# The first forward stage on four 64x64 tiles of the TensorE array, with retuned slots, table rows from PSUM and a last store in halves

## The chip, the cores and the metric

One core of a Trainium2 chip runs the kernel. The metric is device time in microseconds, the median of several executions. Ratios are the mean time of one kernel's runs over that of the other's in the same rounds, so they are not quite the ratio of the medians quoted beside them.

## The reference

```python
X = np.fft.rfft(x, axis=1)                       # x: (8, 3008, 256)
y = np.fft.irfft(X * (filt_r + 1j*filt_i), n=3008, axis=1)
h = y.reshape(24064, 256) @ w_in                 # to 2048
out = (0.5*h*(1 + erf(h/sqrt(2)))) @ w_out       # back to 256
```

The FFT of 3008 = 47 x 64 points is four stages of small matmuls with two trips through DRAM (R1 after the first stage, R2 after the third). The two large matmuls are called ps_h (L450) and ps_o (L464).

## The kernel before: what the argument touches

PSUM is the memory that TensorE writes its results to; it is handed out in banks. Time is planned in slots. A slot holds one ps_h pair (two matmuls of 512 columns) and four ps_o matmuls (256 columns each). The FFT stages of batch b are laid into the slots ahead of hi, the slot in which the large matmuls first need that batch.

```python
def s1(self, b, u):                       # first forward stage, u = 0..15, one a slot
    ...
    ps = self.bank("ps_s1")               # pool "f": 3 PSUM banks for all stages
    nc.tensor.matmul(ps[0:96, :], lhsT=self.T1, rhs=self.st[b, "x"][:, 2*u:2*u+2, :],
                     start=True, stop=True)
    i = (u % 4) * 2
    self._evac(a[:, i:i + 2, :].rearrange("p a b -> p (a b)"), ps[0:96, :], False)   # DVE
    if u % 4 == 3:
        ...                               # two DMAs of a_sb to R1, 192 KB each
...                                       # (cut)
s1, n1, r1, s2, n2, r2, s4, n4 = hi - 94, 1, hi - 78, hi - 69, 3.7, hi - 23, hi - 17, 1
#  s1 first stage; r1 read b_sb from R1; s2 second stage (s3 four slots behind it);
#  r2 read d_sb from R2; s4 last inverse stage
...                                       # (cut)
m.psum(ctx, h=(3, 1), o=(2, 1), f=(3, 1)) # eight banks in all
```

T1 is 94x96 and block diagonal: two halves of the input, 47 rows each, give 48 outputs each, and the other half of the weights is zero.

## Time and profile before

| | before |
|---|---|
| time | 785.1 us (4 runs, 784.36 to 785.24) |
| span of the profiled execution | 781.9 us |
| TensorE busy / share of the last chain | 98% / 93% |
| first forward stage, batches 1 to 7 | 112 matmuls, 220 ns each between starts |
| holes ahead of the last inverse stage | 3.2 us in six batches |

In the views PE is TensorE, PEld its weight loads, DVE VectorE, ACT ScalarE, POOL GpSimd, and SPq the queue from which SyncE issues DMAs. A line has the start, the length, the engine, the line of the kernel, the operation, output<-inputs, the shape and the count; brackets give the idle time just before it and what ended that. A hole is a stretch in which TensorE waits.

The prediction below shows the lines for this. The first is the order of time of the weight loads. The second is the waits: who waited for whom, us in total, times, longest.

```profile
117.50 0.12 PEld L261 LDWEIGHTS <-T 94*96 94x96 bf16 x1
117.72 0.54 PEld L464 LDWEIGHTS <-g_sb 128*128 128x128 bf16 x4
118.27 0.21 PEld L450 LDWEIGHTS <-w_in_sb 128*128 128x128 bf16 x2
```

```profile
PE ps_s L334 <- DMA d_sb<-R: 2.2, 3, 1.8
```

The weights of the first-stage matmul are loaded at 117.50 for a matmul that starts at 117.72. They come one matmul ahead and cost nothing. The wait for d_sb is the only one that TensorE has in the long part.

### The profile page before, as it was taken

The page shows a single profiled execution, that of the slowest core. Times are in us where ns is not written, and L with a number is a line of the kernel's source. Part 1 is how long each engine was busy: PE and PEld are TensorE (multiplying, and loading weights), DVE is VectorE, ACT ScalarE, POOL GpSimd, SP SyncE. Part 2 cuts the span into 40 slices and gives each one's busy share as a digit, 9 for nine tenths or more (in the row PEclk, how much of TensorE's full clock was granted, in tenths as well). Part 3 has the DMA queues.
Part 4 walks back from the last instruction along what each step waited for, and adds up shares of the span by engine and source line. Part 5 has one row for each costly group of instructions (what it writes and reads, how often), then busy time and mean ns, then how long its engine had stood idle before and what let it go on. Part 6 is the DMA issues. An engine that isn't in the chain of part 4 may idle for free.

```text
span 781.9 us, 14728 instructions
## 1 busy us (share of the span) xinstructions
PE 769.3 (98%) x5938; PEld 538.1 (69%) x5938; DVE 403.1 (52%) x720; ACT 567.5 (73%) x978; POOL 64.7 (8%) x155
## 2 busy tenths in 40 slices
PE   8899999999999999999999999999999999999997
PEld 5857676676777766677677776667767677766666
DVE  8866756464554645556454664546645366411011
ACT  6889855887558875588656986568965788666663
POOL 7801100020000100001000110001100000000000
PEclk9999999999999999999999999999999999999999
DMA  9784744465244761546615465254642521410111
GB/s 149 140 179 118 152 123 107 133 134 125 69 109 131 138 149 40 133 130 118 159 44 160 105 123 136 61 168 94 122 135 68 150 81 55 135 41 28 41 42 54
DMA packets 86213, 85.63 MB, mean 110 GB/s; under 512 B 5761, under 2 KB 76417, under 8 KB 86145
## 3 DMA queue, kind: packets, MB, share of 16 engines
q1 hardware_dynamic: 77760, 68.70, 31.0%
q0 software_dynamic: 8384, 16.00, 14.3%
q8 instruction: 46, 0.75, 0.4%
q14 instruction: 23, 0.18, 0.1%
HBM read 54.00 MB, written 46.66 MB: 129 GB/s over the span
## 4 chain that ended last, share of the span: by engine, by line
PE 93%; DMA 3%; POOL 1%; DVE 1%; ACT 0%; issue 0%; SPq 0%; POOLq 0%; DVEq 0%
PE ps_o L464 41%; PE ps_h L450 41%; PE ps_s L261 3%; PE ps_s L334 3%; PE ps_s L309 2%; PE ps_s L284 2%; DMA d_sb<-R 1%; DMA F<-in_filt_i_dram 1%; DMA x_sb<-in_x_dram 1%; PE ps_c3t L413 0%; DMA R<-v_sb 0%; POOL x_sb L82 0%; PE ps_c L427 0%; POOL T L201 0%; ACT vt_sb L246 0%
## 5 line engine op out<-in xcount | busy, mean ns | idle before, releaser
L453 ACT ACTIVATE g_sb<-ps_h 128x512 bf16<-128x512 f32 x752 | 439.1, 596 | 190.3 <-PE ps_h L450 179.5
L464 PE MATMUL ps_o<-w_out_sb,g_sb 128*128 128x256 bf16 x3008 | 449.1, 272 | 0.0
L450 PE MATMUL ps_h<-y_sb,w_in_sb 128*128 128x512 bf16 (+3 forms) x1600 | 447.6, 366 | 0.5 <-DVE y_sb L250 0.5
L464 PEld LDWEIGHTS <-g_sb 128*128 128x128 bf16 x3008 | 287.6, 98 | 133.8
L450 PEld LDWEIGHTS <-w_in_sb 128*128 128x128 bf16 x1600 | 154.9, 98 | 23.3 <-issue 0.8
L468 DVE COPY ost<-ps_o 128x512 f32<-128x512 f32 x94 | 64.3, 684 | 125.2 <-PE ps_o L464 124.7
L292 DVE TENSOR_TENSOR p<-ps_s,F 128x512 bf16<-128x512 f32 x84 | 58.1, 691 | 103.5 <-ACT p L291 97.0
L250 DVE TENSOR_SCALAR y_sb<-ps_s 128x376 bf16<-128x376 f32 x112 | 60.9, 548 | 82.7 <-PE ps_s L334 82.7
L248 DVE CAST a_sb<-ps_s 96x512 bf16<-96x512 f32 x112 | 76.3, 686 | 40.8 <-PE ps_s L261 40.8
L248 DVE CAST v_sb<-ps_s 128x512 bf16<-128x512 f32 x84 | 57.5, 686 | 13.0 <-PE ps_s L309 13.0
L290 ACT ACTIVATE p<-ps_s 64x512 bf16<-64x512 f32 x84 | 49.8, 593 | 2.0
L334 PEld LDWEIGHTS <-d_sb 96*128 96x128 bf16 x448 | 30.3, 97 | 29.0 <-DMA d_sb<-R 3.3
L291 ACT CAST p<-ps_s 64x512 bf16<-64x512 f32 x84 | 48.5, 577 | 1.0
L101 POOL COPY gate<-p 1x1 bf16<-1x1 bf16 x48 | 8.5, 176 | 479.5 <-DVE p L294 479.5
L261 PE MATMUL ps_s<-x_sb,T 94*96 94x512 bf16 x112 | 42.7, 381 | 0.0
L334 PE MATMUL ps_s<-T,d_sb 96*128 96x94 bf16 x448 | 36.3, 204 | 2.3 <-DMA d_sb<-R 2.2
L294 DVE TENSOR_TENSOR p<-p 128x512 bf16<-128x512 bf16 x84 | 35.7, 425 | 2.9
L293 DVE TENSOR_TENSOR p<-p,F 128x512 bf16<-128x512 bf16 x84 | 34.9, 415 | 0.0
L82 POOL DMA_DIRECT2D x_sb<-in_x_dram x64 | 32.6, 515 | 13.0 <-issue 11.3
L309 PE MATMUL ps_s<-p,T 128*128 128x256 bf16 x168 | 32.1, 273 | 0.0
L284 PE MATMUL ps_s<-b_sb,T 128*128 128x256 bf16 x168 | 32.1, 273 | 0.0
L309 PEld LDWEIGHTS <-T 128*128 128x128 bf16 x168 | 16.3, 98 | 20.1 <-DVE p L294 0.5
(98 smaller groups left out, 191.1 us busy)
## 6 DMA issues: line engine op xcount, KB each, us to landing
out_dram<-ost SPq DMA_DIRECT2D x94, 256.0 KB, 2.5
x_sb<-in_x_dram POOLq DMA_DIRECT2D x64, 188.0 KB, 3.9
R<-a_sb SPq DMA_DIRECT2D x56, 192.0 KB, 3.0
b_sb<-R SPq DMA_DIRECT2D x28, 384.0 KB, 4.6
R<-v_sb SPq DMA_DIRECT2D x42, 256.0 KB, 4.0
d_sb<-R SPq DMA_DIRECT2D x56, 192.0 KB, 4.5
w_in_sb<-in_moe_w_in_dram POOLq DMA_DIRECT2D x2, 512.0 KB, 9.9
w_out_sb<-in_moe_w_out_dram POOLq DMA_DIRECT2D x2, 512.0 KB, 10.8
```

The lines of the kernel that those rows point to most:

```text
L248: self.nc.vector.tensor_copy(out=out, in_=in_)
L250: self.nc.vector.tensor_scalar(out=out, in0=in_, scalar1=scale, scalar2=None, op0=ALU.mult)
L261: nc.tensor.matmul(ps[0:96, :], lhsT=self.T1, rhs=self.st[b, "x"][:, 2 * u:2 * u + 2, :], start=True, stop=True)
L290: nc.scalar.activation(out=p2[0:64], in_=ps[64:128], func=AF.Copy, scale=-1.0)
L291: nc.scalar.copy(out=p2[64:128], in_=ps[0:64])
L292: nc.vector.tensor_tensor(out=p1, in0=ps, in1=f(0), op=ALU.mult)
L309: nc.tensor.matmul(ps[:, 256 * i:256 * i + 256], lhsT=self.T3[:, k].rearrange("p a b -> p (a b)"), rhs=w[:, 256 * i:256 * i + 256], start= ...
L334: nc.tensor.matmul(ps[:, 94 * i:94 * i + 94], lhsT=d[:, (grp % 2) * 4 + i, 128 * half:128 * half + 128], rhs=t4, start=True, stop=True)
L450: nc.tensor.matmul(ps[:, o:o + n], lhsT=self.w_in_sb[:, dc, jc * 128:jc * 128 + 128], rhs=self.ring[:, dc, off:off + n], start=(dc == 0), ...
L453: nc.scalar.activation(out=self.st["g", t][:, jc, :], in_=ps, func=AF.Gelu)
L464: nc.tensor.matmul(ps[:, tile_i % 2, :], lhsT=g[:, jc, tile_i * 128:tile_i * 128 + 128], rhs=self.w_out_sb[:, jc, :], start=(jc == 0), sto ...
L468: nc.vector.tensor_copy(out=ost, in_=ps)
```

## The change

The intent is to stop streaming over zeros: 47x48 blocks fit 64x64 tiles, four of which can work at once, so that four matmuls of 512 columns should take little more than one. The slots are retuned around it. Two small parts go with it: the negative table rows of the second half come out of PSUM on ScalarE instead of from GpSimd, and the last output tile is stored in two column halves.

```diff
     def s1(self, b, u):                        # now u = 0..7, one every two slots
+        ps = [self.bank("ps_s1") for h in range(2)]
+        c, i = u // 2, 2 * (u % 2)
+        for r in range(2):
             for h in range(2):
+                w = 8 * c + 4 * r + i
+                nc.tensor.matmul(ps[h][64 * r:64 * r + 64, :], lhsT=self.T1s[64 * h:64 * h + NA],
+                                 rhs=x[64 * h:64 * h + NA, w:w + 2, :], start=True, stop=True)
+        for h in range(2):
+            self._evac(a[:, h, i:i + 2, :].rearrange("p a b -> p (a b)"), ps[h], False)
...  (four DMAs of 96 KB in place of two of 192; x_sb at partitions 0 and 64; T1s built on GpSimd)
+            if h == 1:                         # table_2_swap: negative rows from PSUM
+                self._evac(t2[:, :, 0, 32 * i:32 * i + 32], ..., "act", 2.0 * i - 1.0)
...  (GpSimd copies filters 12 to 15 first, then the small tables, then filters 16 to 23)
+        if last and tile_i == 3:               # mm2: 16 matmuls of 128 columns, store, twice
...
-            s1, n1, r1, s2, n2, r2, s4, n4 = hi - 94, 1, hi - 78, hi - 69, 3.7, hi - 23, hi - 17, 1
+            s1, n1, r1, s2, n2, r2, s4, n4 = hi - 94, 1, hi - 78, hi - 71, 3.5, hi - 26, hi - 17, 1
```

More of the change, by code (lines that the diff above doesn't have):

```diff
@@ L76, in load_x @@
         if lo == 0 and 0 in hs:
-            self.st[b, "x"] = self.px.tile([2 * NA, HB, 256], BF16, tag="x", name="x_sb")
-        xt = self.st[b, "x"]
+            self.st[b, "x"] = self.px.tile([128 if b else 2 * NA, HB, 256], BF16, tag="x", name="x_sb")
+        xt, o = self.st[b, "x"], 64 if b else NA
         xv = self.x[b].rearrange("(n1 h c w) d -> h c n1 w d", h=2, c=4, w=8)
@@ L81, in load_x @@
             for h in hs:
-                nc.gpsimd.dma_start(out=xt[h * NA:(h + 1) * NA, c * 8:c * 8 + 8, :], in_=xv[h, c])
+                nc.gpsimd.dma_start(out=xt[h * o:h * o + NA, c * 8:c * 8 + 8, :], in_=xv[h, c])
     def load_filters(self, k0, k):
@@ L197, in table_2_swap, with table_2_minus @@
                        "act", 1.0 - 2.0 * i)
-    def table_2_minus(self, eng, h):
-        t2 = self.T2[:, 12 * h:12 * h + 12]
-        eng.tensor_scalar(out=t2[:, :, 0, :], in0=t2[:, :, 2, :], scalar1=-1.0, scalar2=None, op0=ALU.mult)
+            if h == 1:
+                self._evac(t2[:, :, 0, 32 * i:32 * i + 32], ps[:, 0:384].rearrange("p (k j) -> p k j", k=12),
+                           "act", 2.0 * i - 1.0)
+    def table_2_minus(self):
+        t2 = self.T2[:, 0:12]
+        self.nc.vector.tensor_scalar(out=t2[:, :, 0, :], in0=t2[:, :, 2, :], scalar1=-1.0, scalar2=None, op0=ALU.mult)
     def weights_4(self, g):
@@ L250, in _evac, with table_1_tiles @@
             self.nc.vector.tensor_scalar(out=out, in0=in_, scalar1=scale, scalar2=None, op0=ALU.mult)
+    def table_1_tiles(self, g):
+        v = self.nc.gpsimd
+        self.T1s = g.tile([128, 64], BF16, name="T1s")
+        v.memset(self.T1s, 0.0)
+        for r in (0, 64):
+            v.tensor_copy(out=self.T1s[r:r + NA, 0:48], in_=self.T1[0:NA, 0:48])
     def s1(self, b, u):
         nc = self.nc
-        if u % 4 == 0:
-            self.st[b, "a"] = self.pa.tile([96, 8, 256], BF16, tag="a", name="a_sb")
+        if u % 2 == 0:
+            self.st[b, "a"] = self.pa.tile([128, 2, 4, 256], BF16, tag="a", name="a_sb")
         if u == 0:
             self.st[b, "R1"] = self.dram.tile([NB, 48, 256], BF16, tag="R1", name="R1")
-        a, R1 = self.st[b, "a"], self.st[b, "R1"]
-        ps = self.bank("ps_s1")
-        nc.tensor.matmul(ps[0:96, :], lhsT=self.T1, rhs=self.st[b, "x"][:, 2 * u:2 * u + 2, :],
-                         start=True, stop=True)
-        i = (u % 4) * 2
-        self._evac(a[:, i:i + 2, :].rearrange("p a b -> p (a b)"), ps[0:96, :], False)
-        if u % 4 == 3:
-            c = u // 4
-            w = R1.rearrange("n q c -> q n c")
-            for h in range(2):
-                nc.sync.dma_start(out=w[:, h * HB + c * 8:h * HB + c * 8 + 8, :],
-                                  in_=a[h * 48:h * 48 + 48, :, :])
+        a, R1, x = self.st[b, "a"], self.st[b, "R1"], self.st[b, "x"]
+        ps = [self.bank("ps_s1") for h in range(2)]
+        c, i = u // 2, 2 * (u % 2)
+        for r in range(2):
+            for h in range(2):
+                w = 8 * c + 4 * r + i
[3 more added lines that the diff above has]
+            self._evac(a[:, h, i:i + 2, :].rearrange("p a b -> p (a b)"), ps[h], False)
+        if u % 2 == 1:
+            o = R1.rearrange("n q c -> q n c")
+            for r in range(2):
+                for h in range(2):
+                    w = HB * h + 8 * c + 4 * r
+                    nc.sync.dma_start(out=o[:, w:w + 4, :], in_=a[64 * r:64 * r + 48, h])
     def r1(self, b, c):
@@ L457, in mm2 @@
         tile_i, q = s // 4, s % 4
+        g = self.st["g", t]
+        last = t == self.B * self.S // TCH - 1
+        if last and tile_i == 3:
+            half = q // 2
+            if q % 2 == 0:
+                self.st["o"] = self.bank("ps_e", "o")
+            ps = self.st["o"][:, 0:128]
+            for jc in range(8 * (q % 2), 8 * (q % 2) + 8):
+                nc.tensor.matmul(ps, lhsT=g[:, jc, 384:512], rhs=self.w_out_sb[:, jc, 128 * half:128 * half + 128],
+                                 start=(jc == 0), stop=(jc == 15))
+            if q % 2 == 1:
+                self.store(t, 3, ps, slice(128 * half, 128 * half + 128))
+            return
         if s % 8 == 0:
@@ L460, in mm2 @@
         ps = self.st["o"]
-        g = self.st["g", t]
         for i in range(4):
@@ L465, in mm2 @@
                              rhs=self.w_out_sb[:, jc, :], start=(jc == 0), stop=(jc == 15))
-        if s % 8 == 7:
+        if last and s == 11:
+            self.store(t, 2, ps[:, 0, :], slice(0, 256))
+        elif s % 8 == 7:
             ost = self.po.tile([128, 2, 256], FP32, tag="ost", name="ost")
@@ L470, in mm2, with store @@
             nc.sync.dma_start(out=self.out[r0:r0 + 256, :].rearrange("(s p) o -> p s o", p=128), in_=ost)
+    def store(self, t, tile_i, ps, cols):
+        ost = self.po.tile([128, 2, 256], FP32, tag="ost", name="ost")
+        o = ost[:, 0, 0:cols.stop - cols.start]
+        self.nc.vector.tensor_copy(out=o, in_=ps)
+        r0 = t * TCH + tile_i * 128
+        self.nc.sync.dma_start(out=self.out[r0:r0 + 128, cols], in_=o)
 @with_exitstack
@@ L520 @@
     m.dup_filters(nc.gpsimd, 4, 8)
-    m.T1p = g.tile([2 * NA, 2, K1, 2], BF16, name="T1p")
-    nc.gpsimd.tensor_copy(out=m.T1p, in_=m.T1.rearrange("p (h r k) -> p h k r", h=2, r=2))
-    m.T1q = g.tile([2 * NA, K1, 2, 2], BF16, name="T1q")
-    nc.gpsimd.tensor_copy(out=m.T1q, in_=m.T1.rearrange("p (h r k) -> p k r h", h=2, r=2))
     warm = g.tile([128, 1], FP32, name="warm")
@@ L534 @@
             m.table_2_swap(0)
-            m.table_2_minus(nc.vector, 0)
+            m.table_2_minus()
             m.warm_up(3)
@@ L552 @@
             m.table_2_swap(1)
-            m.table_2_minus(nc.gpsimd, 1)
-            m.dup_filters(nc.gpsimd, 12, 12)
+            m.dup_filters(nc.gpsimd, 12, 4)
+            m.T1p = g.tile([2 * NA, 2, K1, 2], BF16, name="T1p")
+            nc.gpsimd.tensor_copy(out=m.T1p, in_=m.T1.rearrange("p (h r k) -> p h k r", h=2, r=2))
+            m.T1q = g.tile([2 * NA, K1, 2, 2], BF16, name="T1q")
+            nc.gpsimd.tensor_copy(out=m.T1q, in_=m.T1.rearrange("p (h r k) -> p k r h", h=2, r=2))
+            m.table_1_tiles(g)
+            m.dup_filters(nc.gpsimd, 16, 8)
             m.load_x(1)
@@ L596 @@
         else:
-            s1, n1, r1, s2, n2, r2, s4, n4 = hi - 94, 1, hi - 78, hi - 69, 3.7, hi - 23, hi - 17, 1
+            s1, n1, r1, s2, n2, r2, s4, n4 = hi - 94, 1, hi - 78, hi - 71, 3.5, hi - 26, hi - 17, 1
         for u in range(16):
-            put(s1 + int(u * n1), m.s1, b, u)
+            if u % 2 == 0:
+                put(s1 + int(u * n1), m.s1, b, u // 2)
             put(s4 + int(u * n4), m.s4, b, u // 2, u % 2)
```

## The prediction

> **What bounds the kernel now.** I read the page first, then the waits by releaser, then the order of time in four places: a first-stage window, the start, one inverse stage and the end. TensorE (PE) is the bound: it is busy 98% and carries 93% of the chain that ended last.
>
> ```profile
> PE 769.3 (98%) x5938; PEld 538.1 (69%) x5938; DVE 403.1 (52%) x720; ACT 567.5 (73%) x978; POOL 64.7 (8%) x155
> PE 93%; DMA 3%; POOL 1%; DVE 1%; ACT 0%; issue 0%; SPq 0%; POOLq 0%; DVEq 0%
> L261 PE MATMUL ps_s<-x_sb,T 94*96 94x512 bf16 x112 | 42.7, 381 | 0.0
> L248 DVE CAST a_sb<-ps_s 96x512 bf16<-96x512 f32 x112 | 76.3, 686 | 40.8 <-PE ps_s L261 40.8
> ```
>
> L261 is the first forward stage of batches 1 to 7 (batch 0 takes another way): 112 matmuls that never wait. Half of their stationary operand is zeros, since it is block diagonal. 381 ns is a record that overlaps the next one; the cost is the distance between starts, in the order of time on PE:
>
> ```profile
> 117.29 0.59 PE L450 MATMUL ps_h<-y_sb,w_in_sb 128*128 128x512 bf16 x2
> 117.72 0.38 PE L261 MATMUL ps_s<-x_sb,T 94*96 94x512 bf16 x1
> 117.94 0.60 PE L464 MATMUL ps_o<-w_out_sb,g_sb 128*128 128x256 bf16 x4
> 118.38 0.59 PE L450 MATMUL ps_h<-y_sb,w_in_sb 128*128 128x512 bf16 x2
> ```
>
> One slot (four ps_o, two ps_h) takes 0.87 us; a first-stage matmul adds 0.22 us (117.72 to 117.94). So the stage holds about 112 x 0.218 = 24.4 us of PE's path, and since PE is packed, what leaves PE leaves the end.
>
> From 41 us on, PE has one kind of hole, ahead of the last inverse stage, where d_sb comes back from DRAM just in time or too late:
>
> ```profile
> 191.82 0.59 PE L450 MATMUL ps_h<-y_sb,w_in_sb 128*128 128x512 bf16 x2
> 194.17 0.33 PE L334 MATMUL ps_s<-T,d_sb 96*128 96x94 bf16 x4 [1.76 <-DMA d_sb<-R]
> ```
>
> Only gaps over 150 ns are listed by the profile. By the distance of starts, the ps_h matmul ahead of this stage takes 2136, 342, 486, 616, 604 and 276 ns in batches 2 to 7 where 216 is due: 1.92 + 0.13 + 0.27 + 0.40 + 0.39 + 0.06 = 3.2 us in all.
>
> In batch 1 the picture differs: its first stage runs in the first 16 slots, where there is no ps_o yet, and DVE has its 16 copies end to end, as does ACT nearly with the gelus:
>
> ```profile
> 41.83 9.81 DVE L248 CAST a_sb<-ps_s 96x512 bf16<-96x512 f32 x15 [0.40 <-PE ps_s L261]
> ```
>
> At the start, VectorE waits 1.60 us for GpSimd, which spends 2.14 us on the negative table rows and only then copies the filters:
>
> ```profile
> 21.92 2.14 POOL L201 TENSOR_SCALAR T<-T 128x768 bf16<-128x768 bf16 x1
> 24.13 5.94 POOL L96 COPY F<-F 64x1024 bf16<-64x1024 bf16 x6
> 25.19 5.75 DVE L377 TENSOR_TENSOR p<-ps_c,F 128x1024 bf16<-128x1024 f32 x5 [1.60 <-POOL F L96]
> ```
>
> **What the Trainium skill says.** TensorEngine Tiling (Array Packing), section Key Properties: four 64x64 tiles run independently, but a change of tiling mode drains TensorE. TensorE: Matmul & The Clock Gate, section The mechanism (Part 3): matmuls in different tiles start about 4 ns apart; section Back-to-back issue gap: N/2.4 + 2.5 ns warm, 216 ns for 512 columns. The trace agrees with the last (0.59 us for two ps_h records whose starts lie 0.22 apart); nothing in it shows tiling or a drain. DMA: Bandwidth & Descriptors, section Anatomy of one DMA: about 2 us of a DMA are fixed. The trace agrees: the last 256 KB store takes 2.1 us, and 192 KB of a_sb 3.0 with two in flight.
>
> **The change, part by part.**
>
> First stage. 112 matmuls become 224 of 47 rows by 64 columns, in 56 groups of four that should run together; each group does what two matmuls did in 2 x 218 = 436 ns. Between groups stand ordinary matmuls, so each group pays two changes of mode. Streaming is 216 ns, three more tiles at 4 ns are 12. For a drain I take a guess of my own: the array's 128 rows (the 128*128 of the records) at the pace of the columns, 216/512 ns each, make 54 ns; twice that is about 106. A group is then 216 + 12 + 106 = 334 ns and saves about 100 ns. For the 48 groups of batches 2 to 7: 4.9 us. If changes were free (228 ns) it would be 10.0; if a drain cost the whole overlap of a record (381 - 218 = 163 ns, twice) a group would be 554 and the stage would lose 5.7 us.
>
> Batch 1 gains little of this: there are still 16 copies of about 0.65 us on DVE, two for each group, 10.5 us for the 16 slots, just what they take now, whatever PE does. I allow 0.3 us.
>
> The copies in all stay 112 of 512 columns, now with 128 partitions instead of 96, which costs the same: the 128-partition v_sb copy also takes 686 ns. The writes of a_sb go from 56 of 192 KB to 112 of 96 KB, same packets, twice the issues at some 0.35 us on a queue that is mostly idle.
>
> Slots of the later stages. The read of d_sb moves from 6 to 9 slots ahead of the last inverse stage, and the last middle-stage matmul from 8 to 12 slots ahead of it. That is 12 x 0.87 = 10.4 us for a way that took 194.04 - 185.47 = 8.6 us at its worst (batch 2) and 6.8 us elsewhere. All 3.2 us of these holes should go; I count 3.1.
>
> In exchange the second stage starts 9 slots after the last first-stage group instead of 10 after the last matmul, and closer in time because no first-stage matmul stands in between. In batch 3 now: last copy ends 230.9, writes issued to 231.28 and landed 234.44, read issued 234.57, first part landed 237.84, first use 238.70: 0.86 us to spare. After: the group at 0, copies end near 1.9, four issues to 2.7, landed near 5.2, read landed near 8.5; first use is wanted at 0.33 + 9 x 0.87 = 8.1. I expect a new hole of 0 to 0.5 us in each of six batches; 1.0 us in all, and up to 3 in the bad case.
>
> Start. GpSimd loses the 2.14 us and can copy the next filters when they land (22.56, against a start at 24.13). But its next filters now come after the small table copies, so the third of VectorE's remaining products waits for a copy that ends near 26.9; it begins at 27.5 now. ACT gains two evictions (0.87 us for the like pair at 18.02) in a stretch where it is full from 17.1 to 27.75. Its later gap of 1.16 us takes that up. I count a gain of 0.5 us.
>
> End. Now 0.69 us of copy and 2.1 us of store follow the last matmul at 777.85. The last store becomes 64 KB and its copy 128 columns, some 0.3 us by columns: 0.4 us less, and 0.2 less of store. The last tile becomes 32 matmuls of 128 columns at about 60 ns (sixteen of that width take 0.99 us of loads at 25.13) against 16 at 109: 0.2 us more. Net gain 0.4.
>
> Sum: 785.0 - 4.9 - 0.3 - 3.1 + 1.0 - 0.5 - 0.4 = 776.8.
>
> **Rivals.** (a) The mode changes eat the tiling: a full drain each way, weight loads that can't be fetched ahead across a change, or second column tiles that load only when the first have streamed. For it: nothing in the trace shows a cheap change. Against: the author retuned the slots around this change, which one does for something that pays. Time 781 with a group at the old 436 ns, 787 with 554. (b) The wait for b_sb takes the place of the wait for d_sb: the margin now is 0.86 us and 2 slots are taken from it. At 1 us a batch it makes 782. (c) Tiles run fully together and changes are nearly free, and b_sb lands in time: 785.0 - 10.0 - 0.3 - 3.1 - 0.9 = 770.7. (d) VectorE becomes the bound in the first-stage windows: two copies and the store's copy are 1.54 us for two slots that then take 1.74 + 0.33; this stays below, except in batch 1.
>
> **Range and chances.** 776.8 lies between (c) and (a); I lean slightly to cheap changes and say 776.5, with 770.5 (c) and 784 (most of (a), or (b) with little from the tiles) as the range. Faster by over 2% needs 769.3, which is beyond even (c): 6%. Slower by over 2% needs 800.7, some 16 us lost, for which I see no mechanism: 2%.
>
> **What would show it.** The distance from the first matmul of a group to the next ps_o: near 330 ns right, 430 or more is (a), 230 is (c). The gap before the last inverse stage gone in all six batches. A gap before ps_s<-b_sb of 0 to 0.5 us. Batch 1's copies still end to end. The wait of VectorE for the filter copies at 25 us under 1 us, ACT without its 1.16 us gap. After the last matmul about 2.3 us to the landing of the last store. Most wrong would be the group: each 100 ns of it is 4.8 us.

## The result, and the profile after

The changed kernel takes 782.17 us (4 runs, 781.55 to 782.74) against 785.1. The ratio is 0.9964, with a 95% interval of 0.9947 to 0.9982. The prediction was 776.5, a gain of 8.5 us on the 785.0 that it starts from; 2.9 came.

The page of the changed kernel first: busy times, the last chain by engine, and the copies of the first stage.

```profile
PE 764.2 (98%) x5965; PEld 528.7 (68%) x6066; DVE 400.7 (51%) x722; ACT 568.4 (73%) x980; POOL 63.1 (8%) x157
PE 86%; DMA 7%; POOL 2%; issue 1%; ACT 1%; DVE 1%; SPq 1%; POOLq 0%
L251 DVE CAST a_sb<-ps_s 128x512 bf16<-128x512 f32 x112 | 72.1, 686 | 39.6 <-PE ps_s L277 38.4
```

TensorE's share of the chain fell from 93% to 86%, and DMA's rose from 3% to 7%: 3% of the new chain is the read of b_sb and 1% the writes of a_sb. The chain follows a whole transfer back, so its share is more than what is waited; the waits themselves are measured below. The copies cost 686 ns as before. The order of time on TensorE, in a first-stage window of batch 2:

```profile
118.27 0.59 PE L466 MATMUL ps_h<-y_sb,w_in_sb 128*128 128x512 bf16 x2
118.79 0.41 PE L277 MATMUL ps_s<-x_sb,T1s 47*64 47x512 bf16 x4
119.13 0.61 PE L493 MATMUL ps_o<-w_out_sb,g_sb 128*128 128x256 bf16 x4
```

Two ps_h matmuls that start at 118.27 take 2 x 0.216 us of streaming, so the next matmul is due at 118.70. The group starts at 118.79. Its four records together are 0.41 us long where one alone is 0.40 (the mean in the list of groups): the four tiles do run at once. But the next ps_o starts at 119.13, although 0.216 us of streaming ends at about 119.01. The group holds TensorE from 118.70 to 119.13. Over the 48 groups of batches 2 to 7, the starts and ends in the trace give a median of **93 ns ahead of the group, about 10 ns between its first and last start, and 332 ns from the last start to the next matmul: 436 ns in all**. The two matmuls that a group replaces took 2 x 220 = 440.

The weight loads show the same two edges:

```profile
118.16 0.21 PEld L466 LDWEIGHTS <-w_in_sb 128*128 128x128 bf16 x2
118.79 0.11 PEld L277 LDWEIGHTS <-T1s 47*64 47x64 bf16 x4 [0.42 <-issue]
119.13 0.33 PEld L493 LDWEIGHTS <-g_sb 128*128 128x128 bf16 x4 [0.23 <-issue]
```

Ahead of the group and again behind it, the load starts together with its matmul, not one matmul earlier as at 117.50 in the kernel before. "Issue" says that it waited for no other engine. The copies fit this: in the 42 groups of batches 2 to 7 that follow another, the first copy of the group before, which frees the bank wanted last, ends 1.03 us or more ahead of the group. So the banks and the copies are not what holds it. I call the 93 ns and the time beyond streaming behind the group its edges.

The holes moved. This is the longest one ahead of the second stage of the changed kernel (batch 4), then its waits:

```profile
330.22 0.59 PE L466 MATMUL ps_h<-y_sb,w_in_sb 128*128 128x512 bf16 x2
331.69 0.38 PE L300 MATMUL ps_s<-b_sb,T 128*128 128x256 bf16 x2 [0.87 <-DMA b_sb<-R]
```

```profile
PE ps_s L300 <- DMA b_sb<-R: 1.8, 5, 0.9
```

The views list only gaps over 150 ns. For the whole size I take the distance from the last group of the first stage to the first matmul of the second. Without a wait it is 8.16 us (9.03 in e3 below, which has one slot of 0.87 us more and does not wait). It is 8.49, 8.55, 9.19, 8.56, 8.57 and 8.37 us in batches 2 to 7, so the holes make 2.8 us. The holes ahead of the last inverse stage, 3.2 us before, are gone: the distance from the last third-stage matmul is 10.53 us in all six batches. Batch 4 as an example (the record of the second ps_h is missing; two take 0.43 us):

```profile
383.38 0.38 PE L466 MATMUL ps_h<-y_sb,w_in_sb 128*128 128x512 bf16 x1
383.81 0.33 PE L350 MATMUL ps_s<-T,d_sb 96*128 96x94 bf16 x4
```

At the end, the last copy and the last store, kernel before and then kernel after:

```profile
777.87 0.69 DVE L468 COPY ost<-ps_o 128x512 f32<-128x512 f32 x1 [2.80 <-PE ps_o L464]
778.59 0.37 SPq L470 DMA_DIRECT2D out_dram<-ost  x1
```

```profile
777.74 0.29 DVE L506 COPY ost<-ps_e 128x128 f32<-128x128 f32 x1 [0.60 <-PE ps_e L483]
```

The copy fell from 0.69 to 0.29 us. The store, from issue to landing, fell from 2.12 us (778.59 to 780.71) to 1.53 (778.06 to 779.59). From the end of the last matmul's record to the last landing it is 1.89 us instead of 2.87.

### The profile page after: what moved, and what is told of

It is laid out like the page before. It is cut to its first block, busy times and chain, and to the rows that moved or that the text cites. A ratio compares the mean times of both kernels' runs of the same rounds, so it can differ in the third digit from the quotient of the medians.

```text
span 780.6 us, 14960 instructions
## 1 busy us (share of the span) xinstructions
PE 764.2 (98%) x5965; PEld 528.7 (68%) x6066; DVE 400.7 (51%) x722; ACT 568.4 (73%) x980; POOL 63.1 (8%) x157
## 4 chain that ended last, share of the span: by engine, by line
PE 86%; DMA 7%; POOL 2%; issue 1%; ACT 1%; DVE 1%; SPq 1%; POOLq 0%
PE ps_o L493 40%; PE ps_h L466 36%; PE ps_s L350 3%; DMA b_sb<-R 3%; PE ps_s L277 2%; PE ps_s L300 2%; PE ps_s L325 2%; DMA x_sb<-in_x_dram 2%; DMA R<-a_sb 1%; DMA F<-in_filt_i_dram 1%; POOL x_sb L82 1%; POOL F L96 1%; ACT g_sb L469 1%; SPq L286 1%; DVE a_sb L251 0%
## 5 line engine op out<-in xcount | busy, mean ns | idle before, releaser
L466 PE MATMUL ps_h<-y_sb,w_in_sb 128*128 128x512 bf16 (+3 forms) x1500 | 424.9, 365 | 0.4 <-DVE y_sb L253 0.4
L493 PEld LDWEIGHTS <-g_sb 128*128 128x128 bf16 x2992 | 282.1, 98 | 132.0 <-issue 10.9
L251 DVE CAST a_sb<-ps_s 128x512 bf16<-128x512 f32 x112 | 72.1, 686 | 39.6 <-PE ps_s L277 38.4
L325 PEld LDWEIGHTS <-T 128*128 128x128 bf16 x168 | 16.4, 98 | 20.1 <-DVE p L310 0.5
L300 PEld LDWEIGHTS <-T 128*128 128x128 bf16 x168 | 16.4, 98 | 16.2 <-issue 3.5
```

The costliest lines, as they stand in the source:

```text
L251: self.nc.vector.tensor_copy(out=out, in_=in_)
L300: nc.tensor.matmul(ps[:, 256 * i:256 * i + 256], lhsT=self.T2[:, k, 1:3].rearrange("p a b -> p (a b)"), rhs=self.st[b, "b", k // 6][:, k % ...
L325: nc.tensor.matmul(ps[:, 256 * i:256 * i + 256], lhsT=self.T3[:, k].rearrange("p a b -> p (a b)"), rhs=w[:, 256 * i:256 * i + 256], start= ...
L466: nc.tensor.matmul(ps[:, o:o + n], lhsT=self.w_in_sb[:, dc, jc * 128:jc * 128 + 128], rhs=self.ring[:, dc, off:off + n], start=(dc == 0), ...
L493: nc.tensor.matmul(ps[:, tile_i % 2, :], lhsT=g[:, jc, tile_i * 128:tile_i * 128 + 128], rhs=self.w_out_sb[:, jc, :], start=(jc == 0), sto ...
```

## The experiments

Theory A, formed from the traces: entering and leaving the tiled mode costs as much as the tiles save, and the retuned slots traded one hole for another. The rivals stand in the expectations. All ratios are to the kernel before in the same rounds.

**e1: the first stage put back, the rest of the change kept.**

```diff
-  (four tiles, T1s, x_sb at 0 and 64)
+  (first stage, load of x and its slots as in the kernel before)
-  hi - 94, 1, hi - 78, hi - 71, 3.5, hi - 26, hi - 17, 1
+  hi - 94, 1, hi - 78, hi - 69, 3.5, hi - 24, hi - 17, 1
```

> The changed kernel with its first stage put back (112 matmuls of 94x96, one each slot), the other parts kept; second stage at 69 slots ahead of the batch's first use (two later than in the change) and the read of d_sb at 24, so that neither should wait. Theory A (the group of four tiles costs 436 ns, as much as the two matmuls that it replaces, because entering and leaving the tiled mode costs 94 + 127 ns): the first-stage windows take as long as in the changed kernel, and the time falls by the 2.9 us of holes before the second stage, to about 779.5 us. Rival B (the tiles do save some 100 ns each, and the holes hide it): about 5 us more than A says, 784 or more.

Measured: 780.47 us, ratio 0.9936 (0.9923 to 0.9950). Without the tiles the kernel is as fast, within the intervals, as e3, the tiled one without its holes (0.9930). Its trace has one hole left, 0.6 us for d_sb in batch 2, which explains part of the 1 us above the 779.5 expected. The tiles as built give nothing that can be seen in the time, and rival B falls.

**e2: the slots put back, the tiles kept.**

```diff
-  hi - 71, 3.5, hi - 26
+  hi - 69, 3.7, hi - 23
```

> The changed kernel with the slots of the kernel before (second stage at 69 slots ahead and every 3.7, read of d_sb at 23). A: the holes before the second stage go (2.9 us in the profile of the change) and those before the last inverse stage come back (3.2 us in the profile before), so the time stays at 782.5 +- 1. Rival B' (retuning the slots was the whole gain of 2.9 us): back to 785 or more.

Measured: 783.35 us, ratio 0.9975 (0.9959 to 0.9991), within the expected 782.5 +- 1. No hole ahead of the second stage is left, since b_sb lands 1.0 to 1.6 us early in batches 2 to 7. Those ahead of the last inverse stage are back: its distance is 7.65, 7.84, 7.57, 7.10, 7.51 and 7.21 us, where 7.06 is the least seen in any run with these slots (e8), 2.5 us in all. The retuning mostly moved the wait. What it was worth in sum is not resolved: the medians differ by 1.2 us, but the interval overlaps that of the change (0.9947 to 0.9982).

**e3: second stage, third stage and the read of d_sb one slot later than in the change.**

```diff
-  hi - 71, 3.5, hi - 26
+  hi - 70, 3.5, hi - 25
```

> The changed kernel with the second and third stage and the read of d_sb one slot (0.87 us) later. The way of d_sb has 1.75 to 2.7 us to spare in the trace, the second stage waits 0.22 to 0.42 us in five batches and 1.05 in one. A and its reading of the holes: these fall to 0 and 0.2, the time by some 2.6 us to 779.5. If the holes are no loss (the rival: PE would only wait elsewhere): 782.

Measured: 780.11 us, ratio 0.9930 (0.9918 to 0.9943). One number in the plan removes both holes: b_sb lands 0.22 to 0.65 us before its use, and d_sb too is early. The 2.8 us were real: 0.9964 less 0.9930 makes 2.7 us, and the two intervals do not overlap.

**e4: two groups back to back every four slots in batches 2 to 7.**

```diff
-        ps = [self.bank("ps_s1") for h in range(2)]
+        ps = ... [self.bank("ps_s1", "h" if pair and u % 2 and h else "f") for h in range(2)]
+        if pair and u % 2 == 0:
+            return                               # copies of both groups follow the second
-                put(s1 + int(u * n1), m.s1, b, u // 2)
+                put(s1 + (int(u * n1) if b == 1 else u // 4 * 4), m.s1, b, u // 2, b > 1)
```

> The changed kernel with two groups back to back every four slots in batches 2 to 7, so half the changes of mode; the fourth PSUM bank is borrowed from ps_h, all matmuls and copies are the same. A (the loss is one for each change of mode): eight matmuls take 2 x 216 + 10 + 211 = 653 ns where two groups take 872; 24 x 219 = 5.3 us less, and the copies of the last pair end some 0.8 us sooner, which takes most of the holes before the second stage (2 us): 775. Rival C (the loss belongs to each group: its weights can't be loaded ahead, or its banks come late): 872 ns stay, and only the holes shrink: 780.

Measured: 777.86 us, ratio 0.9903 (0.9889 to 0.9916). The order of time of matmuls, then that of weight loads, in batch 3 (here each ps_h matmul is made in two pieces, of 384 and 128 columns; the slot takes as long):

```profile
214.85 0.60 PE L468 MATMUL ps_h<-y_sb,w_in_sb 128*128 128x384 bf16 x4
215.38 0.63 PE L277 MATMUL ps_s<-x_sb,T1s 47*64 47x512 bf16 x8
215.94 0.61 PE L495 MATMUL ps_o<-w_out_sb,g_sb 128*128 128x256 bf16 x4
```

```profile
215.38 0.14 PEld L277 LDWEIGHTS <-T1s 47*64 47x64 bf16 x8
```

Eight matmuls take 0.56 us from the first start to the next ps_o. With the 93 ns ahead the pair takes 652 ns (median of 24) where two single groups take 872: theory A's 653. Rival C falls: the second group starts 240 ns after the first, where 216 are due, so no edge of that size lies between them, and its weights are loaded with those of the first (all eight loads are over at 215.52). My 775 was missed for another reason. The distance to the second stage is 10.40 to 10.59 us where 9.87 is without a wait (e9's 10.74 less a slot): the holes did not shrink, they grew from 2.8 to 3.75 us, because the last pair's writes of a_sb are issued together behind four copies: the last lands 6.9 us after the second group's start in batch 3, against 5.0 us after the last group's start in the change. So 24 x 0.22 = 5.3 less 1.0 gives 4.3 us; the medians differ by 4.3, the ratios by 0.0061 or 4.8 us.

**e9: pairs and the shift together.** The edits of e4 and e3.

> Pairs of groups, and the second and third stage and the read of d_sb one slot later, for the trace of the pairs showed that the second stage still waits for b_sb in every batch (about 0.3 to 0.7 us each; my expectation that pairs alone would end these holes failed). d_sb has 2.6 us to spare there. Theory A: the holes of some 2.5 us go, 775.4 us. Rival: the wait moves to d_sb or the copies, 777 or more.

Measured: 774.1 us (773.9 to 775.79), ratio 0.9870 (0.9854 to 0.9886). b_sb lands 0.18 to 0.61 us early, and TensorE is 92% of the last chain again. It beats both kernels.

**e8: only the last output tile in halves, on the kernel before.** The diff is that part of the change.

> The kernel before with only the last output tile in column halves. In the profiles the last store landed 1.1 us earlier after PE's last matmul: I expect 784.3 against 785.4, minus 1.1 us. My prediction's term was minus 0.4.

Measured: 784.59 us against 784.46, ratio 0.9998 (0.9985 to 1.0011). Its trace has the shorter end (2.08 us from the last matmul to the landing, 2.87 before), but its first ps_h starts 1.0 us later than in the trace before, with the same code ahead of it. The start varies that much between executions, and this run does not resolve 1 us: the 1.1 us expected did not show. The gain at the end is seen in the traces alone, and not in full in all: the same 64 KB store takes 1.53 us from issue to landing in the change (1.52 to 1.54 in e1, e2, e3, e4 and e9), but 1.72 in e8 and 2.07 in e7.

**e5: one tiny matmul on a 64x64 tile ahead of each first-stage matmul, on the kernel before; e6: the same on the whole array.**

```diff
         ps = self.bank("ps_s1")
+        nc.tensor.matmul(ps[0:64, 0:8], lhsT=self.ones[0:64, 0:64], rhs=self.ones[0:64, 0:8], ...)   # e5
+        nc.tensor.matmul(ps[0:128, 0:8], lhsT=self.ones[:, 0:128], rhs=self.ones[:, 0:8], ...)       # e6
```

> The kernel before with one extra matmul of 8 columns on a 64x64 tile ahead of each of the 112 first-stage matmuls (its output is overwritten by it). Theory A: each costs the two changes of mode, 94 + 117 ns, and little streaming: the distance around it grows by about 215 ns, in all 24 us at most (less in batch 1, whose window is full on DVE): some 805 us. Rival D (the 211 ns belong to four tiles or to their weights, not to the change): under 80 ns each, below 794.

> Control of the extra matmul: the same 8 columns on the whole 128x128 array, no change of mode. Theory A: 20 to 60 ns each, 2 to 7 us in all, 787 to 792. Rival: the same as with the tile, then any small matmul costs that much.

Measured: e5 811.16 us, ratio 1.0348 (1.0324 to 1.0372); e6 787.93 us, ratio 1.0042 (1.0027 to 1.0057). By the ratios that is 27.3 and 3.3 us for 112 matmuls of eight columns, 244 and 29 ns each. Theory A had allowed 24 us at most for e5; what the control costs too makes up the difference, and less the control it is 215 ns. The order of time of e5 and then of e6:

```profile
123.09 0.59 PE L451 MATMUL ps_h<-y_sb,w_in_sb 128*128 128x512 bf16 x2
123.61 0.19 PE L261 MATMUL ps_s<-ones 64*64 64x8 bf16 x1
123.73 0.42 PE L262 MATMUL ps_s<-x_sb,T 94*96 94x512 bf16 x1
123.99 0.38 PE L465 MATMUL ps_o<-w_out_sb,g_sb 128*128 128x256 bf16 x2
```

```profile
119.72 0.59 PE L451 MATMUL ps_h<-y_sb,w_in_sb 128*128 128x512 bf16 x2
120.16 0.17 PE L261 MATMUL ps_s<-ones 128*128 128x8 bf16 x1
120.18 0.40 PE L262 MATMUL ps_s<-x_sb,T 94*96 94x512 bf16 x1
```

With the tile: 0.09 us ahead (due at 123.52, start at 123.61), 0.12 us to the next matmul although eight columns need some 3 ns (an estimate from 216 ns for 512), and the matmul behind it takes 254 ns instead of 220. On the whole array it starts when due and costs 0.03 us. One small tile alone pays edges of the same size, so rival D falls: neither the four tiles nor their data are the reason, but the change of mode.

**e7: row tiles alone (wrong result on purpose); e10: column tiles alone.**

```diff
+        for h in range(2):                                     # e7, on the changed kernel
+            nc.tensor.matmul(ps[h], lhsT=self.T1s[64 * h:64 * h + NA], ...)          # 47 x 128
+        for h in range(2):                                     # e10, on the kernel before
+            nc.tensor.matmul(ps[64 * h:64 * h + 64, :], lhsT=self.T1w[:, 64 * h:64 * h + 64], ...)
```

> The changed kernel with row tiles alone: each group is two matmuls of 47 rows by 128 columns (weights doubled to both column halves, so the output is wrong on purpose, and every second pair of rows is never taken). If any change of tiled shape costs the same (theory A): entry near 94 ns, exit near 117, a group of 216 + 211 = 427 ns. If the columns' halves are what costs (their weights load more slowly): a group near 300.

> The kernel before with each first-stage matmul split into two column halves of 64 on all 94 rows, side by side, result right. Theory A: 216 + 211 ns each instead of 218, so 112 x 209 = 23 us more, some 808 us. If only row tiles change the mode: near 220 ns each, 785.

Measured: e7 782.9 us, e10 808.67 us, both beside a run of 787.32 of the kernel before. The order of time of e7, then of e10:

```profile
118.48 0.59 PE L465 MATMUL ps_h<-y_sb,w_in_sb 128*128 128x512 bf16 x2
119.00 0.39 PE L276 MATMUL ps_s<-x_sb,T1s 47*128 47x512 bf16 x2
119.33 0.61 PE L492 MATMUL ps_o<-w_out_sb,g_sb 128*128 128x256 bf16 x4
```

```profile
120.91 0.59 PE L451 MATMUL ps_h<-y_sb,w_in_sb 128*128 128x512 bf16 x2
121.44 0.41 PE L262 MATMUL ps_s<-x_sb,T1w 94*64 94x512 bf16 x2
121.78 0.61 PE L465 MATMUL ps_o<-w_out_sb,g_sb 128*128 128x256 bf16 x4
```

The whole group takes 418 ns (96 ahead of it) in e7 and 432 (93 ahead) in e10. Both other tile shapes cost about the same, row tiles alone and column tiles alone. The 94x96 matmul of the kernel before, which also leaves part of the array unused, pays none of this (220 ns between starts).

## Why the prediction was wrong, point by point

**First stage: the term that failed.** The prediction put a group at "216 + 12 + 106 = 334 ns", with "a guess of my own" of 54 ns for a drain each way. The 216 and the 12 held (10 ns between the four starts). The 106 for the two changes of mode (twice 54 is 108, a slip) is the term that was mis-sized: the two edges measured 93 and 332 - 216 = 116 ns, 209 in all, so the group is 436 ns against 440: a saving of 0.2 us in 48 groups in place of 4.9. That each group would pay for two changes of mode was right, and rival (a) named it; its size decided everything. That (a) has the very number 436 is luck: it is the old cost of two matmuls, taken as the point of no gain (and (a) then sums to 781.7, not 781). The bound was there too: the trace before gave up to 163 ns for each, and I chose a third of that without a measurement. I also leaned on the author's having retuned the slots, which is no measurement. Whether an edge is the emptying of the array, the weights that are not loaded ahead across it, or both, no run here separates: in every trace they come together. The record of a T1s load is 103 ns long, about as long as an edge, which fits the second reading but does not show it.

**The signs that it named.** The first would have called the group right: from its first matmul to the next ps_o it is 342 ns (median of 48), and "near 330 ns" was to mean right. That distance holds 216 + 10 and only the edge behind, 116; the 93 ns ahead of the group lie outside it. A sign has to span all that a step is to cost. The others came true but for one gap ahead of b_sb (1.03 us in batch 4, 0 to 0.5 said) and the end (1.89 us to the landing, 2.3 said).

**Batch 1.** Counted 0.3 us. From its first ps_h to the first ps_o, 10.21 us before and 10.04 after: 0.2. The copies stay end to end, as said. TensorE is as full there, though: 4 x 216 + 436 = 1300 ns of the 1.31 us from group to group (two copies: 1306), so which of the two sets the pace is not shown. In e5 this stretch grows by 3.7 us, so TensorE has little to spare in it.

**The wait for d_sb.** Counted 3.1, and 3.2 us of holes went. Right.

**The wait for b_sb.** Counted 1.0, measured 2.8: the second term mis-sized. I named it as rival (b) and had it at 0 to 0.5 us for each batch. My own sum said more: a read that lands near 8.5 and is wanted at 8.1 makes 0.4 us a batch, 2.4 in six, and that sum held. Five batches lie 0.21 to 0.41 us above the due 8.16. Only batch 4, with 1.03, is outside: its first read took 4.3 us where the others took 3.4. The 1.0 is not what the working gives. The gain and the loss of the retuned slots cancel but for 0.4 us; e3 shows that both could be had.

**Start.** Counted 0.5. The first ps_h starts at 40.98 us before and 40.81 after. In four traces with the old start (e10, which builds one more table, left out) it lies between 40.98 and 42.01 (mean 41.48), in six with the new one (e7 left out likewise) between 40.81 and 41.39 (mean 41.07): about 0.4, within the scatter. ScalarE's gap of 1.16 us is filled as foreseen.

**End.** Counted 0.4, and the traces show 1.0 us from matmul to landing: the copy 0.40 as said, the store 0.59 instead of 0.2 (see e8 for how it varies). The 32 narrow matmuls cost 0.03 more, not 0.2. The timed e8 does not resolve it.

**The sum** of the parts seen in traces is 0.2 + 0.2 + 3.2 - 2.8 + 0.4 + 1.0 = 2.2 us. The two profiled spans differ by 1.2 us and the timed runs by 2.9, with an interval of 1.4 to 4.2. The profiled execution of the kernel before was its fastest (783.76 us where the others took 784.36 to 785.24), so the spans show too little. How the rest divides between the start and the holes in the executions that were not traced stays open.

**Rivals (c) and (d).** (c) failed, since the mode changes are not free. (d) did not come in batches 2 to 7, as foreseen: there the copies of one group end 0.44 us ahead of the next; in batch 1 it stays open.

## What to carry to other kernels

Tiles of the array do run at once, but each stretch of tiled matmuls among whole-array ones paid about 210 ns here, as much as a whole-array matmul of 512 columns. So tile only in stretches: count changes of mode, not matmuls, and gather groups even if that needs a borrowed PSUM bank (e4, e9). When a stage is moved in a software pipeline, measure the slack on both sides of it, for a hole that is closed on one side can open on the other. An effect on which the sum depends most deserves a measured bound from a one-line kernel such as e5 before it is put into a sum as a guess.

## What the Trainium skill lacked or had wrong

- TensorEngine Tiling (Array Packing), section Key Properties: it says that a change of mode drains TensorE, but gives no size. Here it was 93 ns going in and 116 coming out of 64x64 tiles (e7 with rows alone: 96 and 103; e10 with columns alone: 93 and 120), and the weight loads on both edges start with their matmul instead of one matmul earlier.
- TensorE: Matmul & The Clock Gate, section The mechanism (Part 3): its list says that a weight load overlaps running matmuls only where its row group differs, though the text above the list also allows a load into a background weight buffer. The "only" is too narrow here. In the kernel before, the load at 117.50 runs beside a ps_h matmul on all rows, and in e4 the loads of the second group are over at 215.52 while the first group, on the same rows, streams until about 215.60. The section's 4 ns from tile to tile agrees (10 ns over three steps), but its model of a group leaves out the 209 ns at the edges.
